# Attention kernel: first K load in two interleaved halves, output stores held longer, and part of the last stores put behind the last score fill

## The chip, the cores and the metric

The kernel runs on one core of a Trainium2 chip. The metric is the device time of one execution in microseconds. The core has five engines that run their own instruction streams and meet in semaphores: TensorE (PE, matmul; its weight loads are listed as PEld), VectorE (DVE), ScalarE (ACT), GpSimd (POOL) and SyncE (SP), which here only issues transfers. Sixteen DMA engines move data between the chip's memory (HBM) and the on-chip buffers.

## The reference

Softmax attention without a mask, in bf16, for 16 x 32 = 512 heads with 192 queries, 1024 keys and a head size of 128.

```python
B, H, Sq, Sk, D = 16, 32, 192, 1024, 128
scores = jnp.einsum("bhqd,bhkd->bhqk", q, k) * D ** -0.5
p = softmax(scores, axis=-1)
return jnp.einsum("bhqk,bhkd->bhqd", p, v)
```

## The kernel before, in words

**Quads and fills.** Four heads form a quad; there are NQ = 128 of them, numbered x. Scores are computed transposed, keys on the partitions: a quad has 8 key tiles of 128 keys x 192 queries, so 1536 score columns a head. They are cut into three fills of 512 columns (`CUTS`), so there are NF = 384 fills, numbered f = 3x + b. Each quad also has three output groups, numbered s = 3x + w.

**Path of the inputs.** SP loads K of a quad (1 MB) into `kn`, Q (192 KB) into `qn` and V (1 MB) into `vs`; there are five buffers of each. Partition (a, j) of `kn` holds 32 consecutive key rows of head a, 8 KB. K and Q must be turned so that the head size lies on the partitions. DVE does this by 32 x 32 block transposes of 32-bit words: `turn_k(g)` (L756 to L766) turns one third of a quad's K, with the word blocks `PIECES[b]` = 0 to 6, 6 to 12, 12 to 16 of sixteen, where a block is half a key row; `turn_q(x)` (L768) turns Q. POOL then puts K's pieces in order in `kt` (`order(g)`, L614) and copies V beside columns of ones into `vp` (`spread(x, i)`, L625), so that a matmul with V also gives the row sum.

**The five streams.** PE alternates `qk(f)` (L655, matmuls at L670), which writes the scores of a fill to PSUM, and `pv(f - LAG)` (L678, matmuls at L699), with LAG = 4. A few groups with negative numbers run on cleared data ahead of the first real fill. PE's stream is a hardware loop over two quads, with a straight tail for the last groups. ACT takes the exponential of each fill, once for one head and once for the other three (L861, L864). DVE normalises each output group (`onorm(s)`, L777: reciprocal at L784, multiply at L788 into `ob`). In its loop it does, for each f, `onorm(f - 5)` and then `turn_k(f + 3)`, and `turn_q` once a quad, strictly in that order: an `onorm` stands behind a `turn_k` that waits for K.

**What gates the loads.** SP issues in one written order. The start is staged: K 0; after POOL's second memset (`s_blank`) K 1, Q 1 and half of V 0; after `qk(0)` (`s_qk`) the rest of V 0 and the first half of K 2; after `pv(-3)` (`s_pv`) the second half of K 2, Q 2, V 1, K 3 and so on. Q 0 is issued by ACT on its own queue. Later a K load waits until DVE has turned the K that lay in its buffer, five quads back, and a V load until the output groups have gone on.

**Stores.** Output is stored by pairs of quads (`GQ` = 2, 384 KB a pair) from `NSO` slots of `ob`; the last two quads are stored one by one, the very last in two parts (L527). A pair's store is held back by `HOLD` pairs: ACT issues it after the fill given in `store_at`, which begins at fill 54 and ends at fill 372.

```python
    store_at = {3 * (x + c) + 6 + 6 * HOLD: i for i, (x, c) in enumerate(stores)
                if 3 * (x + c) + 6 + 6 * HOLD <= NF - 12}
```

With HOLD = 7 that gives ACT 54 stores. What is left, nine pairs and the two single quads, SP issues after its last load, each after a wait for the normalisation of its quads. DVE waits for a slot's earlier store before it writes the slot again. At the end DVE checks the row sums, PE and DVE make a flag of that, all engines read it, and a general path that is not taken here would run if it were set. SP waits for all stores (L601) after reading it.

Of the kernel before, what the change touches and what calls it, by code (L numbers as in the profile page):

```python
# [408 lines left out]
U32 = mybir.dt.uint32  # L409
# [12 lines left out]
def _attention_kernel(nc, q, k, v, out):  # L422
# [9 lines left out]
    NF = 3 * NQ  # L432
    LAG = 4

    PRE = 1
# [3 lines left out]
    NKN, NVS, NKT, NVP = 5, 5, 2, 2  # L439
    GQ = 2  # L440

    NSO, HOLD = 10, 7

    HELD = 2
    VB = 136
# [2 lines left out]
    kf = k.rearrange("b h s d -> (b h) s d")  # L448
# [6 lines left out]
    with ExitStack() as outer:  # L455
        redo = outer.enter_context(nc.sbuf_tensor("redo", [1, 1], mybir.dt.int32))

        def sem(name):
            return outer.enter_context(nc.semaphore(name))
# [5 lines left out]
        s_kn = [sem("f_kn%d" % i) for i in range(NKN)]  # L465
# [7 lines left out]
        s_qk = sem("f_qk")  # L473
# [5 lines left out]
        s_pf = sem("f_pf")  # L479
        s_on = sem("f_on")  # L480
        s_fin = sem("f_fin")
        s_held = sem("f_held")
        s_fl = sem("f_fl")

        with ExitStack() as es:  # L485
            def sb(name, shape, dt):
                return es.enter_context(nc.sbuf_tensor(name, shape, dt))
# [5 lines left out]
            kn = sb("f_kn", [128, NKN, 2048], U32)  # L493
# [26 lines left out]
            def store(e, i):  # L520
                so = i % NSO
                x, c = stores[i]
                if x + c == NQ:

                    for y in range(2):
                        e.wait_ge(s_fin, y + 1)
                        e.dma_start(  # L527
                            of[4 * x + 2 * y:4 * x + 2 * y + 2].rearrange("x (p j) d -> (x p) (j d)", j=3),
                            ob[:, so, 3 * y:3 * y + 3, :].rearrange("p j d -> p (j d)"),
                        ).then_inc(s_st[so], 16)  # L530
                    return
                e.wait_ge(s_rc, 3 * (x + c) + 1)
                e.dma_start(
                    of[4 * x:4 * x + 4 * c].rearrange("(a x) (p j) d -> (x p) a (j d)", x=2, j=3),
                    ob[:, so, 0:6 * c, :].rearrange("p (a j) d -> p a (j d)", j=3),
                ).then_inc(s_st[so], 16)


            store_at = {3 * (x + c) + 6 + 6 * HOLD: i for i, (x, c) in enumerate(stores)
                        if 3 * (x + c) + 6 + 6 * HOLD <= NF - 12}  # L540

            def load_q(e, x):
                e.dma_start(
                    qn[:, x % NKN, :],
                    qf[4 * x:4 * x + 4].rearrange("a (j u) d -> (a j) (u d)", u=6).bitcast(U32),
                ).then_inc(s_qn[x % NKN], 16)
# [3 lines left out]
            def hint(eng):  # L550
                hints[eng.engine] = eng.mark_branch_hint_location()

            @block.sync
            def _(e):
                def load_k(x, lo=0, hi=32):
                    if x >= NKN:
                        e.wait_ge(s_kx, 3 * (x - NKN) + 3)
                    e.dma_start(
                        kn[:, x % NKN, 64 * lo:64 * hi],
                        kf[4 * x:4 * x + 4].rearrange("a (j r) d -> (a j) r d", r=32)[:, lo:hi, :]  # L560
                        .rearrange("p r d -> p (r d)").bitcast(U32),
                    ).then_inc(s_kn[x % NKN], 16)

                def load_v(x, lo=0, hi=4):
                    if x >= NVS:
                        e.wait_ge(s_pv, 3 * (x - NVS) + 2 + BLANK)
                    e.dma_start(
                        vs[:, x % NVS, lo:hi, :],
                        vf[4 * x + lo:4 * x + hi].rearrange("a (m t) d -> m a (t d)", t=T),
                    ).then_inc(s_v[x % NVS], 16)  # L570


                load_k(0)
                e.wait_ge(s_blank, 1)
                load_k(1)
                load_q(e, 1)
                load_v(0, 0, 2)
                e.wait_ge(s_qk, PRE + 1)
                load_v(0, 2, 4)
                load_k(2, 0, 16)  # L580
                e.wait_ge(s_pv, BLANK - 2)
                load_k(2, 16, 32)
                load_q(e, 2)
                for n in range(3, NKN):
                    load_v(n - 2)
                    load_k(n)
                    load_q(e, n)
                for n in range(NQ):
                    if n == NQ // 2:
                        hint(e)  # L590
                    if n + NKN - 2 < NQ:
                        load_v(n + NKN - 2)
                    if n + NKN < NQ:
                        load_k(n + NKN)
                        load_q(e, n + NKN)
                for i in range(len(store_at), len(stores)):
                    store(e, i)
            def stored(e):
                for so in range(NSO):
                    last = (len(stores) - 1) % NSO == so  # L600
                    e.wait_ge(s_st[so], 16 * (len(range(so, len(stores), NSO)) + last))  # L601
# [132 lines left out]
            def _(dve):  # L734
# [21 lines left out]
                def turn_k(g):  # L756
                    x, b = divmod(g, 3)
                    lo, hi = PIECES[b]
                    if b == 0:
                        dve.wait_ge(s_kn[x % NKN], 16 * (x // NKN + (2 if x % NKN == 2 else 1)))  # L760
                    if x >= 2:
                        dve.wait_ge(s_qk, 3 * (x - 2) + b + 1 + PRE)
                    dve.transpose(  # L763
                        kx[:, x % 2].rearrange("p (U s j u) -> p s u U j", s=2, j=32, u=2)[:, :, :, lo:hi],
                        kn[:, x % NKN].rearrange("p (s u U i) -> p s u U i", s=2, u=2, i=32)[:, :, :, lo:hi],
                    ).then_inc(s_kx, 1)  # L766
# [37 lines left out]
                def check(lo, hi, i, part):  # L804
# [9 lines left out]
                    dve.wait_ge(s_dv, cnt[0])  # L814

                turn_k(0)
                turn_q(0)
                for g in range(1, 5):
                    turn_k(g)
                turn_q(1)  # L820
                for f in range(NF + LAG + 1):
                    s = f - LAG - 1
                    if f == NF // 2:
                        hint(dve)
                    if s >= 0:
                        onorm(s)
                        if 0 <= s - EARLY < 3:
                            check(0, 2 * EARLY, 0, s - EARLY)
                    g = f + AHEAD
                    if 5 <= g < NF:  # L830
                        x, b = divmod(g, 3)
                        if b == 2 and x >= 2:
                            turn_q(x)
                        turn_k(g)
# [36 lines left out]
def bass_standalone__mha_softmax__near_ridge_kernel(  # L871
    nc: bass.Bass,
    q: bass.AP,
    k: bass.AP,
    v: bass.AP,
    out: bass.AP,
):
    _attention_kernel(nc, q, k, v, out)
# [28 lines left out]
```

## Time and profile before

| What | Value |
|---|---|
| Time, median of 3 runs | 814.06 us (813.41 to 814.98) |
| Span of the profiled execution | 812.8 us |
| Mean granted PE clock | 0.997 |
| PE busy, DMA moved | 98%, 393 GB/s on average |
| K load, issue to landing (median of 127) | 18.0 us |
| V load, issue to landing (median of 127) | 16.2 us |
| Pair stores issued by ACT / by SP | 54 / 9 |
| First / last store issued by ACT | 124.9 us / 778.5 us |
| Last pair stores issued by SP | 778.69 to 800.69 us |

A line of a view that runs in order of time gives the start, the duration, the engine, the line of the program, the operation with output and input, the count, and in brackets how long the engine had been idle before and what ended that. A line of a view by stage gives the stretch, its length, then for each engine the busy time and the number of instructions, then the clock granted to PE, the mean share of time in which the 16 DMA engines were busy, and what they moved. In the page the row of DMA digits shows that share in forty equal slices, in tenths.

### The profile page before, as it was taken

How to read it: one execution, taken by the hardware profiler on the slowest of the kernel's cores; microseconds unless marked ns; L12 is line 12 of the kernel's file. 1: busy time of each engine (PE TensorE's matmuls, PEld its weight loads, DVE VectorE, ACT ScalarE, POOL GpSimd, SP SyncE). 2: the span in 40 equal slices, each digit the busy share in tenths (PEclk: the TensorE clock that was granted, in tenths of full speed). 3: DMA queues.
4: the chain of work that ended last, by engine and by line, in shares of the span. 5: the costliest groups of instructions: out<-in, count | busy, mean ns of one | idle time of the engine just before them, and what ended most of it. 6: DMA issues, size and time to landing. Idle time of an engine off the chain costs nothing. (4 is left out here: it accounts for less than half of the span.)

```text
span 812.8 us, 71452 instructions
## 1 busy us (share of the span) xinstructions
PE 800.4 (98%) x32996; PEld 714.3 (88%) x32996; DVE 599.3 (74%) x1293; ACT 749.9 (92%) x772; POOL 551.6 (68%) x648
## 2 busy tenths in 40 slices
PE   8999999999999999999999999999999999999996
PEld 6888888888888888888888888888888888888885
DVE  4777777777777777777777777777777777778773
ACT  6899999999999999999999999999999999999994
POOL 5676676676677667667667766766766776667762
PEclk9999999999999999999999999999999999999999
DMA  7999999999999999999999999999999999999995
GB/s 265 406 397 403 399 402 402 409 405 404 409 405 405 408 405 405 407 406 405 406 406 405 406 407 407 405 407 405 403 408 398 400 394 405 376 407 403 384 366 166
DMA packets 138474, 319.20 MB, mean 393 GB/s; under 512 B 7232, under 2 KB 56384, under 8 KB 122176
## 3 DMA queue, kind: packets, MB, share of 16 engines
q1 hardware_dynamic: 109776, 297.36, 93.7%
q10 hardware_dynamic: 28656, 21.43, 7.8%
q14 instruction: 35, 0.29, 0.1%
q8 instruction: 7, 0.11, 0.1%
HBM read 293.60 MB, written 25.17 MB: 392 GB/s over the span
## 5 line engine op out<-in xcount | busy, mean ns | idle before, releaser
L864 ACT ACTIVATE f_pt<-f_s 128x1536 bf16<-128x1536 f32 x384 | 554.9, 1445 | 0.0
L620 POOL COPY f_kt<-f_kx 128x768 uint32<-128x768 uint32 (+1 forms) x384 | 300.8, 787 | 212.4 <-DVE f_kx L763 212.3
L699 PE MATMUL f_o<-f_vp,f_pt 128*64 128x129 bf16 x12368 | 426.2, 222 | 1.6 <-PEq L653 1.4
L670 PE MATMUL f_s<-f_qt,f_kt 32*128 32x192 bf16 (+1 forms) x20528 | 422.8, 226 | 2.9 <-PEq L653 2.2
L699 PEld LDWEIGHTS f_o<-f_vp,f_pt 128*64 128x64 bf16 x12368 | 362.8, 110 | 50.6 <-issue 23.8
L670 PEld LDWEIGHTS f_s<-f_qt,f_kt 32*128 32x128 bf16 x20528 | 348.6, 92 | 39.4 <-issue 3.8
L763 DVE STREAM_TRANSPOSE f_kx<-f_kn 128x768 uint32<-128x768 uint32 (+1 forms) x384 | 333.8, 870 | 14.1 <-DMA f_kn<-in_k_dram 13.6
L629 POOL COPY f_vp<-f_vs 128x1024 uint32<-128x1024 uint32 x256 | 259.8, 1044 | 35.1 <-DMA f_vs<-in_v_dram 32.5
L861 ACT ACTIVATE f_pt<-f_s 128x512 bf16<-128x512 f32 x384 | 229.2, 597 | 51.5 <-PE f_s L670 8.1
L784 DVE RECIPROCAL f_rinv<-f_o 128x2 f32<-128x2 f32 x381 | 64.7, 170 | 178.2 <-PE f_o L699 178.1
L788 DVE TENSOR_TENSOR f_ob<-f_o,f_rinv 128x256 bf16<-128x256 f32 x381 | 161.6, 424 | 13.0
L772 DVE STREAM_TRANSPOSE f_qt<-f_qn 128x384 uint32<-128x384 uint32 x128 | 72.9, 570 | 0.0
L699 PE MATMUL f_s<-f_vp,f_pt 128*64 128x129 bf16 x96 | 3.3, 220 | 1.6 <-issue 1.5
L699 PEld LDWEIGHTS f_s<-f_vp,f_pt 128*64 128x64 bf16 x96 | 2.9, 110 | 1.9 <-issue 1.6
L848 ACT ACTIVATE f_pt<-f_ones 128x1536 f32<-128x1536 bf16 x3 | 4.2, 1472 | 0.0
L608 POOL MEMSET f_vp<- 128x1088 uint32 (+1 forms) x3 | 3.8, 1309 | 0.0
L848 ACT ACT_TABLE_LOAD x1 | 1.3, 1283 | 1.2 <-PEq L892 1.2
L784 DVE RECIPROCAL f_rinv<-f_s 128x2 f32<-128x2 f32 x3 | 0.5, 171 | 2.6 <-PE f_s L699 2.5
L712 PE MATMUL f_o<-f_ones 128*128 128x512 bf16 x2 | 1.0, 620 | 1.1 <-POOL f_ones L605 1.1
L736 DVE MEMSET f_pt<- 128x256 uint32 x4 | 1.1, 272 | 0.9 <-PEq L892 0.9
L729 PE MATMUL f_o<-f_bad,f_ones 128*1 128x1 bf16 x1 | 0.2, 165 | 1.4 <-DVEq L837 1.4
L788 DVE TENSOR_TENSOR f_ob<-f_s,f_rinv 128x256 bf16<-128x256 f32 x3 | 1.3, 425 | 0.3 <-DVE f_rinv L784 0.3
(15 smaller groups left out, 5.3 us busy)
## 6 DMA issues: line engine op xcount, KB each, us to landing
f_kn<-in_k_dram SPq DMA_DIRECT2D x127, 1024.0 KB, 18.0
f_vs<-in_v_dram SPq DMA_DIRECT2D x127, 1024.0 KB, 16.2
f_qn<-in_q_dram SPq DMA_DIRECT2D x127, 192.0 KB, 14.2
out_dram<-f_ob ACTq DMA_DIRECT2D x54, 384.0 KB, 9.6
out_dram<-f_ob SPq DMA_DIRECT2D x9, 384.0 KB, 7.2
f_vs<-in_v_dram SPq DMA_DIRECT2D x2, 512.0 KB, 6.1
f_kn<-in_k_dram SPq DMA_DIRECT2D x2, 512.0 KB, 5.6
f_qn<-in_q_dram ACTq DMA_DIRECT2D x1, 192.0 KB, 5.9
```

The costliest lines, as they stand in the source:

```text
L608: return gp.memset(part.bitcast(U32), 0x3F803F80)
L620: gp.tensor_copy(kt[:, x % NKT].bitcast(U32).rearrange("p U (j s u) c -> p U j s (u c)", s=2, u=2)[:, lo:hi], kx[:, x % 2].rearrange("p (U ...
L629: gp.tensor_copy(vp[:, x % NVP, 2 * T * i: 2 * T * i + 2 * T, 0:D].bitcast(U32), vs[:, x % NVS, 2 * i: 2 * i + 2, :].rearrange("p a (t d) ...
L670: ins = pe.matmul(S[:, c0: c0 + n1 - n0], kt[r, x % NKT, 2 * t + h, :, c], qt[r, x % R, h, n0:n1, c], start=w == 0 and g == 0, stop=w == 3 ...
L699: ins = pe.matmul(O[64 * z: 64 * z + 64, u, 0:129], pt[:, x % R, 2 * y + z, t * SQ + 64 * j: t * SQ + 64 * j + 64], vp[:, x % NVP, (2 * y ...
L763: dve.transpose(kx[:, x % 2].rearrange("p (U s j u) -> p s u U j", s=2, j=32, u=2)[:, :, :, lo:hi], kn[:, x % NKN].rearrange("p (s u U i) ...
L772: dve.transpose(qt[:, x % R].bitcast(U32).rearrange("p b (y j u) c -> p u y b (j c)", y=3, u=2), qn[:, x % NKN].rearrange("p (u y b i) -> ...
L784: dve.reciprocal(ri, O[:, :, 128]).then_inc(s_rc, 1)
L788: ins = dve.tensor_tensor(ob[:, so, 6 * a + 2 * w: 6 * a + 2 * w + 2, :], O[:, :, 0:128], ri.unsqueeze(2).to_broadcast([128, 2, D]), ALU.mult,
L848: return act.activation(part.bitcast(F32), ones[:, 0:1].to_broadcast([128, 2 * T * SQ // 2]), ACT_FN.Copy)
L861: act.activation(pt[:, x % R, 0, c], s1_ps[:], ACT_FN.Exp, scale=scale).then_inc(s_e1, 1)
L864: act.activation(pt[:, x % R, 1:4, c], s3_ps[f % 2][:], ACT_FN.Exp, scale=scale).then_inc(s_e3, 1)
```

## The change

There are three parts. First, K of quad 0 is loaded by two transfers of 512 KB that interleave: within each partition's 32 key rows the first takes four of every eight rows (runs of 1 KB), the second the other four. The first counts on a semaphore of its own, `s_k0`. `turn_k(0)` reads only word blocks 0 to 6, which lie in the first half's rows, and waits for that alone; `turn_k(1)` waits for the second. The purpose is that the first transpose can begin before the whole K has landed.

Second, stores are held nine pairs behind in place of seven, with twelve output slots in place of ten. ACT then issues 52 stores, from fill 66 on, and SP eleven pairs and the two single quads. The purpose is that loads meet fewer stores.

Third, of those last stores SP issues four pairs at once, and then waits for the last score fill (`s_qk` at NF + PRE) before the seven others. The purpose is that the stores don't fill the DMA engines in the last fills.

```diff
-    NSO, HOLD = 10, 7
+    NSO, HOLD = 12, 9
...
+        s_k0 = sem("f_k0")
...
-                load_k(0)
+                for i in range(2):
+                    e.dma_start(
+                        kn[:, 0].rearrange("p (s z w) -> p s z w", s=4, z=2)[:, :, i],
+                        kf[0:4].rearrange("a (j s z r) d -> (a j) s z (r d)", s=4, z=2, r=4)[:, :, i].bitcast(U32),
+                    ).then_inc(s_kn[0] if i else s_k0, 16)
                 e.wait_ge(s_blank, 1)
...
                 for i in range(len(store_at), len(stores)):
+
+                    if i == len(store_at) + 4:
+                        e.wait_ge(s_qk, NF + PRE)
                     store(e, i)
...
                 def turn_k(g):
                     x, b = divmod(g, 3)
                     lo, hi = PIECES[b]
-                    if b == 0:
+                    if g == 0:
+                        dve.wait_ge(s_k0, 16)
+                    elif b == (x == 0):
                         dve.wait_ge(s_kn[x % NKN], 16 * (x // NKN + (2 if x % NKN == 2 else 1)))
```

## The prediction

> **What bounds the kernel now.** I read the page first (parts 1 and 2), then the busy time by stage, the start and the end in order of time, the waits, and last the semaphore landings of each load.
>
> ```profile
> PE 800.4 (98%) x32996; PEld 714.3 (88%) x32996; DVE 599.3 (74%) x1293; ACT 749.9 (92%) x772; POOL 551.6 (68%) x648
> DMA  7999999999999999999999999999999999999995
> ```
>
> TensorE and the DMA engines are both full from the second slice on, so the middle has two limits that lie almost on each other. By stage (PE, PEld, DVE, ACT, POOL busy, clock, DMA share, GB/s):
>
> ```profile
> 0.00:8.64 8.64, 5.60 (x98) 4.02 (x98) 4.33 (x9) 5.51 (x4) 5.00 (x9) 1.00 0.78 285
> 8.64:28.87 20.23, 18.30 (x688) 16.14 (x689) 10.05 (x18) 15.53 (x16) 10.88 (x13) 0.92 0.88 319
> 28.87:800.70 771.83, 771.26 (x32055) 689.53 (x32054) 581.21 (x1253) 726.89 (x750) 535.77 (x626) 1.00 1.03 400
> 800.70:812.80 12.10, 5.22 (x162) 4.66 (x162) 3.68 (x14) 1.94 (x2) 0.00 (x0) 0.97 0.33 99
> ```
>
> From 28.87 to 800.70 PE idles 0.57 us in all: a score fill and an output group (qk and pv) pass every 2.054 us, and nothing there can be won but that half microsecond. What is left is the first 29 us and the last 12. The start, in order of time:
>
> ```profile
> 5.16 1.73 PE L699 MATMUL f_o<-f_vp,f_pt 128*64 128x129 bf16 x32
> 6.48 0.98 DVE L763 STREAM_TRANSPOSE f_kx<-f_kn 128x768 uint32<-128x768 uint32 x1 [3.24 <-DMA f_kn<-in_k_dram]
> 7.52 0.85 POOL L620 COPY f_kt<-f_kx 128x768 uint32<-128x768 uint32 x1 [2.77 <-DVE f_kx L763]
> 8.67 1.10 PE L670 MATMUL f_s<-f_qt,f_kt 32*128 32x192 bf16 x48 [1.78 <-PEq L653]
> ...
> 9.71 1.77 PE L699 MATMUL f_o<-f_vp,f_pt 128*64 128x129 bf16 x32
> ...
> 26.11 0.98 DVE L763 STREAM_TRANSPOSE f_kx<-f_kn 128x768 uint32<-128x768 uint32 x1 [2.09 <-DMA f_kn<-in_k_dram]
> ...
> 27.84 1.10 PE L699 MATMUL f_o<-f_vp,f_pt 128*64 128x129 bf16 x32 [1.39 <-PEq L653]
> ```
>
> K of quad 0 lands at 6.45 (its semaphore's sixteenth count), and DVE, POOL and PE follow in a chain of 2.19 us to the first real fill at 8.67. PE is empty from 6.89. Then the same output group that takes 1.10 us elsewhere takes 1.77: a half clock. At 27.84 PE waits for onorm(2), which stands on DVE behind turn_k(9), which waits for K of quad 3 (landed 26.09). After that PE never waits long again, so the finish of the loop is the landing of K 3 plus a constant. The end:
>
> ```profile
> 802.86 0.42 DVE L788 TENSOR_TENSOR f_ob<-f_s,f_rinv 128x256 bf16<-128x256 f32 x1
> 804.42 1.97 PE L699 MATMUL f_s<-f_vp,f_pt 128*64 128x129 bf16 x63 [1.46 <-issue]
> ```
>
> PE stands still for 1.46 us, waiting for nothing in the program. The packet records show a 16 KB instruction packet at 802.14 that took 0.95 us; PE resumes 1.33 us after its end, as at 17.84 after a packet that ended at 16.51. So it is an instruction fetch that came late: stores had filled the engines at about 320 GB/s from 796.6 to 802.6.
>
> One more reading, from the landings: K of quad x lands before DVE takes it by 0.0 us at x = 3, 0.7 at 6, 5.7 at 18 (the stores begin at 124.9), 4.5 at 60, 1.9 at 108, and 0.0 to 0.6 from 118 on. The stores eat the lead. At the end V arrives just in time too: V 118 lands at 744.06 and its copy delays the score fill at 748.25 by 0.52 us.
>
> [...] the clock is 0.50 from 9.94 to 13.35[...]. [...] from 2.7 to 5.5 us Q's 1.5 KB packets on ACT's queue alternate with K's 8 KB ones. [...] 8 KB took 309 ns, 2 KB 84, 1.5 KB 65. [...]
>
> **The change part by part.**
>
> *K 0 in halves.* The first half (512 KB, even groups of four key rows) is all that turn_k(0) reads; turn_k(1) waits for the second. A 1 KB packet is not in the trace; the line through 309, 84 and 65 ns gives about 46 ns (estimate). Before, an engine moved 8 packets of 309 = 2.47 us of K and 8 of 65 = 0.52 us of Q from 1.84 on, plus a slow first packet (some 0.5 us more) and 0.35 us from last packet to semaphore: 5.7, against a first count at 5.83 and a last at 6.45. After: 32 x 0.046 = 1.49 in place of 2.47, so the last count comes near 5.3 at best; at worst, if strided 1 KB reads are slow, where it was (6.4). I take 5.2 to 5.4. Q 0 lands earlier, since it alternates with short packets. The second half lands near 6.8, while turn_k(0) and turn_q(0) keep DVE until about 6.8: its wait costs nothing. The whole K 0 takes 0.5 us more of DMA time, which delays K 1 (10.19 to about 10.7); turn_k(3) uses that, and fill 3 then stands some 3 us off. Extra SP issue, 0.4 us: hidden before the wait for s_blank (2.9).
>
> First fill: 8.67 - 1.2 = 7.4 to 7.5. PE's hole shrinks from 1.78 to about 0.6 us, [...] and the clock should stay full. That takes 0.68 + 0.83 us from the next two fill-to-fill distances (2.74 and 2.89 against 2.05). So pv(-3), which releases the second half of K 2 (SP issue 14.41), comes 2.7 us earlier, and qk(0), which releases V 0's second half and K 2's first (9.80), 1.2 earlier. In between the DMA was not full: the share over 10 to 19 us is 0.31 to 0.84, 2.8 us of idle engine time in sum. Most of that goes; 0.5 us comes back by the shorter packets. K 3 lands 2 to 3 us earlier; I take **2.6**, from 1.2 (clock still drops) to 3.5 (all idle time gone). PE's own path gains up to 4, so K 3 still decides.
>
> *Two more pairs held.* Can the DMA keep up with a PE that is 2.6 us ahead? Its own start moves by as much. And two stores fewer (2 x 1.2 us at 320 GB/s) go before the last loads: 2.4 us of lead at the end. So quads 118 to 127 are no longer just in time, and the 0.52 us at 748.25 goes: **-0.5**. The ACT queue loses two issues of 0.38 us, not on the path. Slots of ob: 12 for 9 held keeps the same distance of three pairs.
>
> *The wait before the last stores.* Queued behind it on SP are seven pair stores and the last quads' stores, nothing else; who waits for them is the end of the program. The first four go out in the quiet before. PE's late fetch then meets empty engines (at 10.33, with the engines a third busy, it came at once), so the 1.46 us hole and the 0.24 after it close: PE and DVE end 1.7 us earlier against the last fill. But 7 x 0.393 + 0.393 = 3.14 MB now begin only at the last fill's end (800.70 in the old time) + 0.9 from issue to data, and at 320 GB/s take 9.8 us: they end at 811.4, land at about 811.9, where the last store before landed at 809.6 and SP's final waits were passed at 811.1. SP's last issue, pressed back by full queues, comes near 809.4 where it was 808.0. So SP takes the end over from DVE: the program ends 0.3 us before to 1.0 us after the old time, relative to the last fill. I take **+0.3**: the fetch is won and the stores give it back.
>
> Sum: -2.6 - 0.5 + 0.3 = -2.8 us; 814.06 - 2.8 = **811.3**.
>
> **Rivals.**
>
> *The start gives little.* Strided 1 KB reads cost more than the line says (the half loads of K 2, 4 KB of every 8, showed packets of 159 ns but also 250 ns on average from 15 to 19 us), or the clock drops all the same. Then K 3 comes 1.2 us earlier: -1.2 - 0.5 + 0.3 gives 812.7. For it: everything but K 0 is still 400 GB/s work. Against: the hole before the first fill must shrink, and the half clock followed that hole.
>
> *The end gains as well.* If the last stores drain faster than 320 GB/s or SP's end is shorter than I think, most of the 1.7 us stays: -2.6 - 0.5 - 1.2 gives 809.8. Against: 320 GB/s was steady for 6 us.
>
> *Slower.* K 0 lands no earlier, the store burst also delays the instruction fetches after the final branch (8 KB packets at 810.8 to 811.7), and the end is 1.8 us later with nothing won at the start (0.2 us lost): 814.06 + 2.0 = 816.1. For it: the burst does lie over those fetches. Against: it needs both parts to fail.
>
> **How the numbers follow.** Forecast 0.60, small start 0.20, end gains 0.12, slower 0.08. 0.2% is 1.6 us: faster means below 812.4. Nearly all of the forecast's case (0.57), all of the third (0.12) and a little of the second (0.04) are faster: 0.73. Same: 0.19; slower: 0.08. The range leaves out the slow case and the tails: 809.4 to 813.4.
>
> **What would show it.** Right: first DVE transpose near 5.3, first real fill near 7.4, no clock of 0.50 around 10 to 13 us, K 3 landed by 23.5, a lead of over 2 us for K 118 and later, no hole in PE's last output groups, and stores at 320 GB/s for 8 to 10 us after the last fill, with SP last. Wrong: K 0's half landing at 6 or later; a half clock; a PE wait in the middle where the DMA fell behind; or an end that follows PE (gain kept) or ACT's branch fetch (loss).

## The result and the profile after

The changed kernel takes 817.24 us (817.13 to 817.83), the kernel before 814.11 (813.41 to 814.98) beside it: a ratio of 1.0039, 95% interval 1.0022 to 1.0057. It is slower by about 3 us, where 2.8 us less were forecast. The profiled spans, 815.5 against 812.8, differ by as much. Where the 2.7 us lie in these two executions is read from two marks, the first matmul of `qk(8)` and that of the last fill:

| | before | after | difference |
|---|---|---|---|
| start of the span to `qk(8)` | 28.87 | 30.62 | +1.75 |
| `qk(8)` to the last fill | 770.71 | 770.65 | -0.06 |
| last fill to the end | 13.18 | 14.26 | +1.08 |

The table is one execution of each. In the six profiles of kernels that load K 0 whole (the one before and five below), `qk(8)` begins anywhere from 28.45 to 31.32 us, so the +1.75 alone proves no loss at the start; that rests on the repeated runs of the next section.

The page's busy times and its row of DMA shares are those of before to the last digit or nearly, so they don't show in the middle that anything was changed:

```profile
PE 800.5 (98%) x32996; PEld 714.4 (88%) x32996; DVE 599.1 (73%) x1293; ACT 749.9 (92%) x772; POOL 552.3 (68%) x648
```

By stage, cut at the same events as before (first real fill, `qk(8)`, end of the last fill; columns as before):

```profile
0.00:7.05 7.05, 5.66 (x98) 4.06 (x99) 3.61 (x8) 5.51 (x4) 5.00 (x9) 1.00 0.73 230
7.05:30.62 23.57, 18.45 (x688) 16.18 (x688) 11.01 (x18) 15.26 (x16) 10.89 (x13) 0.93 0.83 303
30.62:802.39 771.77, 771.34 (x32055) 689.55 (x32054) 580.77 (x1253) 727.14 (x751) 536.38 (x626) 1.00 1.03 398
802.39:815.46 13.07, 5.09 (x162) 4.65 (x162) 3.68 (x14) 1.94 (x2) 0.00 (x0) 0.88 0.79 246
```

The first stage is 1.6 us shorter, and the second 3.3 us longer, with the same 688 matmuls in it. In the last stage the DMA share went from 0.33 to 0.79. The start in order of time:

```profile
4.86 0.98 DVE L773 STREAM_TRANSPOSE f_kx<-f_kn 128x768 uint32<-128x768 uint32 x1 [1.62 <-DMA f_kn<-in_k_dram]
...
7.05 1.04 PE L678 MATMUL f_s<-f_qt,f_kt 32*128 32x192 bf16 x44
8.67 0.24 PE L678 MATMUL f_s<-f_qt,f_kt 32*128 32x128 bf16 x4 [0.58 <-issue]
...
11.56 0.93 PE L707 MATMUL f_o<-f_vp,f_pt 128*64 128x129 bf16 x26
15.70 0.36 PE L707 MATMUL f_o<-f_vp,f_pt 128*64 128x129 bf16 x6 [3.21 <-issue]
...
17.06 1.94 PE L707 MATMUL f_o<-f_vp,f_pt 128*64 128x129 bf16 x32
...
27.87 0.98 DVE L773 STREAM_TRANSPOSE f_kx<-f_kn 128x768 uint32<-128x768 uint32 x1 [1.42 <-DMA f_kn<-in_k_dram]
...
29.59 1.10 PE L707 MATMUL f_o<-f_vp,f_pt 128*64 128x129 bf16 x32 [0.73 <-PEq L661]
```

K 0's half lets DVE begin at 4.86 (before 6.48), and the first fill comes at 7.05 (8.67), both 0.3 us or more earlier than forecast. Then PE stops twice in the middle of a group, released by nothing of the program ("issue"): after 44 of the 48 matmuls of `qk(0)`, and for 3.21 us after 26 of the 32 of `pv(-3)`. Before, both groups ran through. The half clock (0.50 from 17 to about 20 us, 1.94 us for a group) now comes behind that hole. K 3 lands at 27.84, where 26.09 was before.

What the DMA engines did meanwhile (by stage, one microsecond each; the last number is GB/s):

```profile
10.00:11.00 1.00, 0.47 (x33) 0.50 (x37) 0.15 (x1) 0.90 (x1) 0.81 (x2) 1.00 1.02 350
11.00:12.00 1.00, 1.00 (x60) 0.90 (x51) 1.00 (x2) 0.32 (x1) 0.11 (x1) 1.00 1.08 406
...
13.00:14.00 1.00, 0.00 (x0) 0.00 (x0) 0.74 (x2) 0.62 (x1) 0.03 (x1) 1.00 0.47 178
14.00:15.00 1.00, 0.00 (x0) 0.00 (x0) 0.00 (x0) 0.00 (x0) 1.00 (x2) 1.00 0.04 16
15.00:16.00 1.00, 0.30 (x8) 0.21 (x10) 0.00 (x0) 0.00 (x0) 1.00 (x3) 1.00 0.00 0
```

The same view of the kernel before, where they had run out of released loads for a moment:

```profile
10.00:11.00 1.00, 1.00 (x26) 1.00 (x22) 0.79 (x1) 1.00 (x2) 0.27 (x1) 0.50 0.31 93
```

The next lines show the packets by queue (number, MB, share of the sixteen engines), the first from 8.7 to 13.3 us, when no other queue moved anything, the second from 13.3 to 14.4:

```profile
q1 hardware_dynamic: 803, 1.73, 100.8%
...
q8 instruction: 1, 0.02, 5.5%
```

In the packet records this instruction packet of 16 KB, which comes just before the hole ends, starts at 13.38 and takes 0.96 us; PE resumes 1.36 us after its end. Before, the packet for the same place in the code started at 10.33, in that moment of 93 GB/s. The new order of the loads has no such moment until 13.4. From 14 to 17 us the DMA engines then stand all but empty, because the second half of K 2 waits for `pv(-3)`, which PE cannot finish (SP issues it at 16.10; before 14.41).

The end, in order of time:

```profile
802.40 7.82 SPq L534 DMA_DIRECT2D out_dram<-f_ob  x8
...
803.22 3.27 PE L707 MATMUL f_s<-f_vp,f_pt 128*64 128x129 bf16 x96
...
809.03 0.15 DVE L849 CAST redo<-f_o 1x1 int32<-1x1 f32 x1 [0.34 <-PE f_o L738]
810.26 1.94 SPq L528 DMA_DIRECT2D out_dram<-f_ob  x2
```

PE runs through (96 matmuls in 3.27 us), and DVE's last cast is 7.76 us after the last fill began. But SP's last stores are issued at +8.99 and +10.30 and so it reaches the first meeting of the engines at +11.27, where it was DVE at +10.13 before.

### The profile page after: what moved, and what is told of

It reads as the page before. It is cut to its first block, busy times and chain, and to the rows that moved or that the text cites. A ratio compares the mean times of both kernels' runs of the same rounds, so it can differ in the third digit from the quotient of the medians.

```text
span 815.5 us, 71453 instructions
## 1 busy us (share of the span) xinstructions
PE 800.5 (98%) x32996; PEld 714.4 (88%) x32996; DVE 599.1 (73%) x1293; ACT 749.9 (92%) x772; POOL 552.3 (68%) x648
```

## The experiments

Each is a change to the kernel before, unless it says otherwise. A profile is one execution. Of 63 executions of the kernel before, beside the first runs here, most lie within 2 us of their median, but they range from 812.5 to 820.6 us. So times are compared by the ratios of repeated runs, and profiles for what happens inside.

**K 0 in halves, nothing else.** The first part of the change: `s_k0`, the two transfers and `turn_k`'s waits.

```diff
-                load_k(0)
+                for i in range(2):
+                    e.dma_start(
...
+                    ).then_inc(s_kn[0] if i else s_k0, 16)
...
-                    if b == 0:
+                    if g == 0:
+                        dve.wait_ge(s_k0, 16)
+                    elif b == (x == 0):
```

> Kernel before with K of quad 0 in two interleaved halves, nothing else. Theory A (instruction fetch): the first fill starts near 7.05 as in the changed kernel, PE then stands about 3 us inside an output group (after 26 of its 32 matmuls) because the 16 KB instruction packet comes near 13.4 in place of 10.3; K 3 lands near 27.8, the last fill starts about 1.7 us later than before, the end is the old one: 815.8 us (815.3 to 816.3). Rival B (the loss of the change is in its end alone): first fills gain or keep, 813.0 to 814.3.

816.89 against 814.41, ratio 1.0023 (1.0011 to 1.0035): slower by 1.9 us. `pv(-3)` stops after 26 matmuls for 3.56 us, and the packet starts at 13.67. The halves change nothing but the start, so the start's loss belongs to this part alone.

**Two more pairs held, and the wait before the last seven.**

```diff
-    NSO, HOLD = 10, 7
+    NSO, HOLD = 12, 9
...
+                    if i == len(store_at) + 4:
+                        e.wait_ge(s_qk, NF + PRE)
```

> Kernel before with 9 pairs held, 12 slots and the wait ahead of the last seven pair stores; K of quad 0 in one load. If the end costs what the two profiles say (from the start of the last fill to the end 14.26 us in place of 13.18): no hole in PE's last output groups, SP's last issue near 12 us after the last fill's start, 815.2 us (814.7 to 815.7). Rival (all of the loss is at the start): 814.1 or, with the hole closed, down to 812.5.

816.38, ratio 1.0018 (1.0005 to 1.0031). From last fill to end it takes 14.25 us, as in the changed kernel (14.26); in the twelve profiles without this wait of seven stores it takes 11.4 to 13.9. The excess of this and of the halves add up to 0.41%, the whole change's is 0.39%.

**Two more pairs held, no wait.** Only the first line of that diff.

> Kernel before with 9 pairs held and 12 slots, no wait: eleven pair stores follow the last load at once. Theory: the lead of the loads is capped by five buffers near 7 us before the stores begin, so holding more brings no more than 1 us of lead at quad 118 and no time; two more stores (1.2 us each) at the end push the late instruction packet and PE's hole back by up to 2.4 us: hole 1.5 to 4 us, 814.1 to 816.5 us. Rival (the forecast's step): lead of 2 us and more at quad 118, 813.5 us.

815.64, ratio 1.0006 (0.9990 to 1.0021): no difference that can be told. The hole at the end that was expected was 0.37 us here, not 1.5. The cap of 7 us on the lead of the loads (landing of K to its use by DVE) was wrong too. The lead grows until the first store is issued, at 124.9 us in the kernel before and at 152.5 us here, and then shrinks again:

| lead of K, us | quad 18 | quad 27 | quad 118 |
|---|---|---|---|
| before | 5.66 | 7.26 | 0.31 |
| nine pairs held, no wait | 6.84 | 9.92 | 3.62 |
| nine pairs held, wait before three stores (below) | 5.66 | 8.84 | 3.32 |
| changed kernel | 3.98 | 7.22 | 1.35 |

In the second row PE started later, which alone is worth some 1.5 us (2.20 at quad 6 against 0.68 before); the third row starts like the first. So the hold gave the lead that the prediction counted on (2.4 us), and some more. V, which was just in time before (0.05 us from quad 110 on), was 1.8 us early or more here. But the lead bought no time that can be told. In the changed kernel's profile part of it was lost before any store (quad 18), for a reason that no run here looked into.

**The kernel before once more**, beside the runs above.

> The kernel before once more, unaltered, for its profile alone. The two runs with its start (one load of K 0) had their last fill start at 803.1 where the first profile had 799.6. If that is the spread of the start from execution to execution, this one lies anywhere from 799.5 to 803.5, and the difference sits in the landing of K 3 (26 to 28 us) and the fill distances behind it; the stretch from the last fill's start to the end is 12.8 to 13.2 us with PE's hole of 1 us or more.

814.43, one execution; from last fill to end 11.90 us with no hole in PE (its packet came 0.92 us after the last fill began, where it was 2.56 in the profile shown with the prediction). So the hole of 1.46 us that the wait was to close is not in every execution.

**The wait before the last three stores only.** HOLD stays 7.

```diff
+                    if i == len(store_at) + 6:
+                        e.wait_ge(s_qk, NF + PRE)
```

> Kernel before with the wait for the last score fill ahead of the last three pair stores alone (seven pairs held, as before). Theory: the quiet lets PE's instruction packet come 0.9 us after the last fill's start, no hole, and three stores of 1.25 us drain before the end needs SP: from the last fill's start to the end about 11.7 us in place of 13.1, so 812.7 us where before is 814.1 (0.9983 of it). Rival (any wait there makes SP the last): 13 us or more, no gain or a loss.

813.50, ratio 0.9995 (0.9982 to 1.0009): no difference that can be told, where 0.9983 was expected. The end in order of time:

```profile
801.28 3.49 PE L701 MATMUL f_s<-f_vp,f_pt 128*64 128x129 bf16 x96
...
805.46 1.41 SPq L527 DMA_DIRECT2D out_dram<-f_ob  x2
...
807.30 0.15 DVE L841 CAST redo<-f_o 1x1 int32<-1x1 f32 x1 [0.34 <-PE f_o L732]
```

SP's last two issues now lie ahead of DVE's cast, and the end is 11.68 us after the last fill began, against 14.25 with seven stores behind the wait. The same with nine pairs held and twelve slots:

> Kernel before with nine pairs held in twelve slots and the wait ahead of the last three pair stores alone. Theory: holding more brings no lead that lasts, so it equals the run with seven held and the same wait, within 0.5 us. Forecast's step (two more pairs held are worth up to 0.5 us in the middle): 0.5 us less. If eight stores don't drain before the last fill: a hole as in the kernel before, 1 us more.

813.42, ratio 0.9992 (0.9982 to 1.0002). The number of stores behind the wait is what costs; the hold again adds nothing, though K of quad 118 lands 3.32 us ahead of its use and V 1.7 us. Near 746 us PE waits all the same:

```profile
743.69 1.07 DVE L809 TENSOR_SCALAR f_chk<-f_rinv 128x702 f32<-128x702 f32 x1
...
744.80 0.58 DVE L774 STREAM_TRANSPOSE f_qt<-f_qn 128x384 uint32<-128x384 uint32 x1
...
745.83 1.10 PE L672 MATMUL f_s<-f_qt,f_kt 32*128 32x192 bf16 x48 [0.68 <-PEq L655]
```

The first line is the first of three steps of DVE's check of the row sums; it stands in DVE's stream ahead of the turning of Q (second line) that this fill, number 357, needs. Against the usual 2.054 us from fill to fill, fills 357 to 360 lose 1.18 us here, 0.70 in the kernel before, and 0.64 to 1.26 in every profile, whether the loads are early or not. That the check is the cause is read from the order on DVE; no run moved it.

**Halves, the loads behind them released later** (added to the halves alone: K 1, Q 1 and V 0 wait for `qk(0)`).

```diff
                 e.wait_ge(s_blank, 1)
+                e.wait_ge(s_qk, PRE + 1)
...
-                e.wait_ge(s_qk, PRE + 1)
```

> K of quad 0 in halves, and K 1, Q 1 and the first half of V 0 issued only after the first fill, so that the DMA engines are empty when PE asks for its next instructions; stores as before. Theory A: the second early instruction packet comes within 1.5 us of PE's reaching the block's first instruction, not 4.7 us, and PE's hole inside the output group falls from 3.2 us to under 1 us; K 1 and all after it land later, so the time need not fall. Rival C (the hole is PE waiting for data or a semaphore): the hole stays or grows, since every load but K 0 comes later.

816.09, ratio 1.0018 (1.0008 to 1.0028). The hole did not shrink: it is 4.11 us and the packet starts at 13.78. The expectation was wrong, and at first sight this speaks against the fetch, since the engines were empty while PE ran on from the border in `qk(0)` at 8.86:

```profile
9.00:10.00 1.00, 1.00 (x36) 0.93 (x32) 0.00 (x0) 0.85 (x2) 0.63 (x2) 1.00 0.00 0
```

But after a stop the next packet takes its time even in empty engines: 1.42 us in the changed kernel (PE goes on at 15.70, packet at 17.12), 1.40 in the halves alone. So it was due here at about 10.3 (an estimate from these two), and the first packets of K 1, issued at 9.21, came at 10.20. From 11 to 14 us the engines moved 350 to 420 GB/s. That the fetch came just too late and waited behind these loads fits the times; it is argued, not shown.

**Halves, and a quiet DMA at the start**: everything behind K 1 waits for `pv(-3)`.

```diff
                 load_k(1)
+                e.wait_ge(s_pv, BLANK - 2)
...
-                e.wait_ge(s_qk, PRE + 1)
...
-                e.wait_ge(s_pv, BLANK - 2)
```

> K of quad 0 in halves; K 1 as before, but Q 1, all of V 0 and K 2 issued only after pv(-3), so that nothing but K 0 and K 1 is in the DMA engines when PE asks for the instructions that follow its first fill. Theory A: the second early 16 KB packet comes before 11 us (13.4 to 13.8 so far with halves) and PE's hole inside pv(-3), 3.2 to 4.1 us so far, falls under 1 us; V 0 lands 2 to 3 us later, so the time may be worse (814 to 817). Rival C (a data wait, or a fetch that comes at a fixed distance): the hole stays above 2.5 us.

The packet starts at 11.24, right after K 1 has landed (11.09), and `pv(-3)` runs through. The late data cost more, with PE waiting 2.34 and 2.46 us for it: 818.93, ratio 1.0063 (1.0040 to 1.0086).

**Halves, second half of K 2 released earlier.**

```diff
-                e.wait_ge(s_pv, BLANK - 2)
+                e.wait_ge(s_qk, PRE + 2)
```

> K 0 in halves alone, but the second half of K 2 is released by the end of qk(1) (about 11.6 us) in place of the end of pv(-3) (16.0). Theory A (PE's instruction fetch waits behind queued loads, and the hole it makes in pv(-3) then holds back K 2): the hole in pv(-3) stays, since the fetch was queued before, or grows by as much as the added loads are ahead of it (3.2 to 5 us); but the engines don't stand empty from 14 to 17 us, and K 3 lands 1 to 3 us earlier than in the kernel with halves alone (25 to 27). The next block boundary, in qk(3), may show a hole now. Time between 814.4 and 816.9. Rival: the empty engines cost nothing, since DVE is held up elsewhere: K 3 lands at 27.8 or later and the time stays at 816.9.

817.34, ratio 1.0032 (1.0021 to 1.0044): slower than expected. In its profile the hole has moved on by one block, into `qk(3)`:

```profile
9.88 0.27 PE L675 MATMUL f_s<-f_qt,f_kt 32*128 32x128 bf16 x4 [1.96 <-issue]
...
16.69 0.98 PE L675 MATMUL f_s<-f_qt,f_kt 32*128 32x192 bf16 x39
20.52 0.50 PE L675 MATMUL f_s<-f_qt,f_kt 32*128 32x128 bf16 x9 [2.85 <-issue]
```

The first stop was longer here (packet at 7.46), the next loads were released later, the engines fell to 131 GB/s from 11 to 12 us, and the second packet got through at 11.57: no hole in `pv(-3)`, against the expectation. K 3 landed at 25.29, earlier than in the kernel before, and PE never waited for it. Even so `qk(8)` came at 31.38: 6.1 us after K 3 landed, where it is 2.8 us in the kernel before. So an earlier K 3 was worth nothing here, while PE stood for 1.96 and 2.85 us at borders.

**Halves, the loop's code moved against the blocks.** `head_slot` 226 becomes 236, then 128 and 16; nothing else changes.

```diff
-                             head_slot={mybir.EngineType.PE: 226}):
+                             head_slot={mybir.EngineType.PE: 236}):
```

> K 0 in halves alone, with the loop's code placed so that every block boundary of PE's instructions comes 10 instructions, 5 matmuls, earlier. Theory A (fetch): the stops move with it: qk(0) stops after 39 of 48 matmuls and pv(-3) after 21 of 32, of much the same length (3 to 4 us), and the 16 KB packet stands before the end of the hole by 1.3 to 1.4 us. Rival (a semaphore, the data of pv(-3), or the clock): pv(-3) still stops after 26 matmuls, or at a group's start.

PE's line of time, slot 236:

```profile
7.03 0.98 PE L675 MATMUL f_s<-f_qt,f_kt 32*128 32x192 bf16 x39
8.94 0.34 PE L675 MATMUL f_s<-f_qt,f_kt 32*128 32x128 bf16 x9 [0.92 <-issue]
...
11.27 0.81 PE L704 MATMUL f_o<-f_vp,f_pt 128*64 128x129 bf16 x21
14.20 0.53 PE L704 MATMUL f_o<-f_vp,f_pt 128*64 128x129 bf16 x11 [2.12 <-issue]
```

Both stops moved by exactly five matmuls, from 44 to 39 and from 26 to 21. No wait and no data of the program moved, so the stop is at a border of the code. The size was expected at 3 to 4 us and is 2.12, as this time the packet got in at 11.68. A third stop, of 3.81 us at 24.65, follows at a later border. This was one execution (818.80 us), so it says nothing of the time.

> K 0 in halves alone, boundaries 98 instructions, 49 matmuls, earlier: the first then lies in the empty group before the first fill (pv(-5) after 27 of 32 matmuls, about 6 us), the second in qk(1) after about 41 of 64. Theory A: PE asks for the second block from about 6 us on, in place of 8.7, when only K 0's second half and K 1 are ahead of it; the packet comes by 9 to 11 and the hole of 3 us goes or falls below 1 us; the half clock after it goes, K 3 lands at 24 to 26, and the time is 812 to 814.5. Rival within A: the packet waits for the end of the burst (13.4) wherever it is asked, and the hole is in qk(1), 4 us or more. Rival: the hole isn't a fetch, pv(-3) still stops and the time is 816.9.

The direction of this shift was taken wrongly: a smaller slot puts the borders later in the code, here by 48 matmuls. The second border is then in `qk(2)`:

```profile
12.36 1.00 PE L675 MATMUL f_s<-f_qt,f_kt 32*128 32x128 bf16 x42
16.22 0.34 PE L675 MATMUL f_s<-f_qt,f_kt 32*128 32x192 bf16 x6 [2.86 <-issue]
```

`pv(-3)` has no stop and releases K 2 at 12.46, so the engines aren't empty (280 GB/s from 14 to 15 us), and K 3 lands at 24.15. PE still stops, for 2.86 and later 1.51 us, and `qk(8)` is at 31.11. 816.48, ratio 1.0013 (0.9995 to 1.0030): the gain that was expected (812 to 814.5) did not come.

> K 0 in halves alone, boundaries 210 instructions, 105 matmuls, earlier: the first in the first empty fill (about 3.9 us), the second in pv(-4) after about 17 of 32 matmuls (9.3 us), the third in qk(2) after about 14 of 48 (13 us). Theory A: the second block's packet comes at 6 to 7 us as the first one did, so neither qk(0) nor pv(-3) stops; the third is asked for from 9.3 us into full queues and comes at 13.4 or later, so qk(2) stops after about 14 matmuls for 2 us or more. Time 813 to 817. Rival: the hole stays in pv(-3).

The borders came 23 matmuls earlier than in the halves alone. `pv(-3)` stops after 3 of 32 for 1.16 us, and the fourth border is the worst that was seen:

```profile
18.71 1.09 PE L675 MATMUL f_s<-f_qt,f_kt 32*128 32x64 bf16 x62
25.99 0.34 PE L675 MATMUL f_s<-f_qt,f_kt 32*128 32x192 bf16 x2 [6.19 <-issue]
```

PE had passed the border before at 17.00, and the packet started at 23.62. The packets by queue in the time between (packets, MB, share of the sixteen engines):

```profile
q1 hardware_dynamic: 749, 1.95, 92.0%
```

and in the next 1.2 us, when it came:

```profile
q1 hardware_dynamic: 176, 0.42, 93.6%
q8 instruction: 1, 0.02, 5.1%
```

820.93, ratio 1.0074 (1.0053 to 1.0095), with not one transfer, wait or matmul different from the halves alone (1.0011 to 1.0035). So stops at the borders cost time by themselves. The same shifts were not tried on the kernel that loads K 0 whole.

## Why the prediction was wrong, point by point

**The half load, the first fill: right.** 4.86 and 7.05 against 5.2 to 5.4 and 7.4 to 7.5; packets of 1 KB took 46 ns (median), as estimated. Q 0 landed at 3.33, K 0's second half at 8.31 (forecast 6.8); that delays `turn_k(1)`, and `qk(1)` waits 0.60 us for it.

**"Most of that goes; ... K 3 lands 2 to 3 us earlier": wrong, and this is the step that failed.** The idle DMA time around 10 us was counted as loss to be won back. It was the time in which PE's second block of instructions was fetched (the 16 KB packet at 10.33). From stop to stop lie some 126 matmuls with their weight loads (4 + 32 + 64 + 26 in the changed kernel), and PE runs through them in some 3 us. The packet itself takes about 1.0 us (0.93 to 1.36 at the start of the kernel before and of the changed kernel) and PE goes on 1.2 to 1.7 us after it, so it has to start within about half a microsecond to one microsecond of the moment when PE enters the block before (an estimate from these durations). Where the engines had room it did: entered at 9.5, packet at 10.33 (before). With the loads that the halves bring forward it started 4.7 us after entry. In the six profiles of kernels with K 0 whole this packet started between 9.95 and 10.50, with the engines 13 to 40% busy from 10 to 11 us, and `pv(-3)` stopped for 0.4 us at most. With halves and the same placement of the code it was 13.38 in the changed kernel, 13.67 with the halves alone and 13.78 with the loads released later, with stops of 3.2 to 4.1 us. It came at 11.2 to 11.6, without a stop, only where the engines had room before it (the quiet start, and the earlier release of K 2).

K 3 came 1.75 us later in place of 2.6 earlier: a step that is 4.3 us off. Some of that is chance, as K 3 landed between 25.67 and 27.70 in the six profiles with K 0 whole; with halves and the same placement and releases it was 27.84 and 28.94. And "the finish of the loop is the landing of K 3 plus a constant" failed with it: with K 2 released earlier K 3 landed at 25.29, and the last fill still began 2.9 us later than before.

The prediction had the fact in hand: it used the late fetch for the end of the program and named the packet "at 10.33, with the engines a third busy, it came at once". It did not ask what the start's packets would meet once the engines were full. At the start PE stopped for up to 6.2 us at a border (slot 16). The kernel before and the changed kernel show seven 16 KB packets each, on queue q8: four by 25 us and three from 802 us on. In no profile here is there one from 46 us until the last fill, and in these two PE has no stop with the releaser "issue" from 46 to 800 us.

**"The clock should stay full": wrong in its consequence.** The stretch after the first fill stayed full (1.00 from 7.05 to 16.9 us), but behind the hole of 3.21 us the half clock came a few microseconds later (0.50 from 17 to about 20 us). That the length of a hole decides this was the author's estimate and is not shown: with slot 236 the clock stayed at 1.00 from 14 to 19 us behind a hole of 2.12 us. In the kernel before, the half clock stretched PE's work from 10 to 13 us (groups of 1.77 and 1.89 us in place of 1.10 and 1.09) and so gave the fetch more time. It isn't needed for that: with nine pairs held and the wait before three stores PE ran there at full clock, the packet came at 10.31, and `pv(-3)` stopped for 0.37 us.

**The hold, -0.5: the lead came, the time did not.** The 2.4 us of lead were right (3.0 more at quad 118 in the run that starts like the kernel before), though the changed kernel's profile kept only 1.0 of it. What failed is the next link, that "the 0.52 us at 748.25 goes" once the loads are early. Fills 357 to 360 lost 0.64 us in the changed kernel against 0.70 before, and 1.17 and 1.18 where both K and V were well ahead: in those profiles PE waits for DVE instead, which has the check of the row sums to do just there. A gain of 0.5 us, if there were one, would also be less than these runs can tell.

**The end, +0.3: right mechanism, size +1.08.** PE's fetch was won (no hole, DVE's cast 1.6 us nearer to the last fill), SP took over, and the stores ran at 300 to 333 GB/s (forecast 320). The term that was too small is SP's last issue: +10.30 after the last fill began in place of +9.8, and it takes 0.63 us where 0.34 was, with the engine's drain (0.13 us) behind it. The sum is just above what was given for this step (+1.0). That the hole wasn't in every execution makes the part won smaller still in the median. Of the two parts at the end only the wait before seven stores shows a cost: 1.0018 with it (interval above 1), 1.0006 without (interval with 1 inside). The two intervals overlap, but the profiles agree: 14.25 us from last fill to end against 12.20.

**The rival "slower"** had the right side for another reason. It supposed that K 0 lands no earlier and that nearly all the loss is at the end. K 0's half did land earlier; the start lost time (0.23% in repeated runs), and so did the end (0.18%).

What stays open: why the packet found a place at 11.68 among full engines with slot 236, and not before 13.4 in the three others. No run set the queues at the moment of asking by themselves, and none kept the halves and their loads and let the packet through early. So that the stops cost time is shown by the shifted code, and that they are all of the 0.23% is not.

## What to carry to other kernels

Before idle DMA time is won back, look at what small transfers use it: here an instruction packet of 16 KB that started 3 us later stopped PE for as long. Stops with the releaser "issue", in the middle of a group and at the same matmul count in every execution, were such borders, and a shift of the code by a few instructions proved it. More lead for the loads was worth nothing where something else held the engine up at the same place (K 3.32 us early at quad 118, ratio 0.9992; 0.9995 without the hold). Stores put behind a wait at the end should drain before the last engine is done: three of them showed no cost here, seven cost 0.18%.

## What the runs showed of the hardware

- After a stop at a border and with all but empty DMA engines, the packet for the block behind the next border started 1.40 to 1.42 us after PE went on (changed kernel, halves alone, slot 236). With loads moving it was 1.6 to 6.6 us (both with slot 16). In the changed kernel 1.73 MB of loads passed from 8.7 to 13.3 us and no instruction packet among them.
- PE resumed 1.23 to 1.71 us after the packet's end, at every stop of this kind in the fourteen profiles.
- The packets of the load with runs of 1 KB took 46 ns (median), those of 8 KB 309 ns; half of K 0 was there for DVE 1.6 us before the whole had been (4.86 against 6.48), the second half landed at 8.31 (the whole at 6.45).
- The placement of one loop's code alone moved the time from 816.5 to 820.9 us.
